# Moving small GpSimd and VectorE operations between steps of a fused SSD and gated-FFN kernel

## The chip, the cores and the metric

The kernel runs on one core of a Trainium2 chip. The metric is the device time of one execution in microseconds (us), lower is better; the time quoted is the median of several runs. A core has five engines with a queue of instructions each: TensorE (PE, matmuls; PEld is its weight load), VectorE (DVE), ScalarE (ACT), GpSimd (POOL) and SyncE (SP, which issues nearly all transfers here). Each engine works through its queue in order and waits on semaphores for the others.

## The reference

Two blocks follow each other. The first is a chunked state-space scan over `x` (4 sequences, 8 heads, 768 positions, head size 32) with decays `a` and rows `B`, `C` (state size 16):

```python
for c in range(nc):                      # chunks of 32 positions
    la = log_a[:, :, sl]
    cum = np.cumsum(la, axis=-1)
    L = np.exp(cum[:, :, :, None] - cum[:, :, None, :]) * causal
    M = np.einsum('bhin,bhjn->bhij', Cc, Bc) * L
    y_intra = np.einsum('bhij,bhjd->bhid', M, xc)
    y_inter = np.einsum('bhin,bhnd->bhid', Cc, state) * np.exp(cum)[:, :, :, None]
    y[:, :, sl] = y_intra + y_inter
    Bx = np.einsum('bhjn,bhjd->bhjnd', Bc, xc) * np.exp(cum[:, :, -1:] - cum)[:, :, :, None, None]
    state = decay_full[:, :, None, None] * state + np.sum(Bx, axis=2)
```

Its output, seen as 3072 tokens of 256 features, goes through the second block:

```python
h = x @ w_in                             # 256 -> 2048
g = h * np.cos(h)
return (g @ w_out).astype(np.float32)    # 2048 -> 256
```

All of it is in float32.

## The kernel before

The sequence of 768 positions is cut into six chunks of 128 (`NC`), each for all four sequences, so a chunk is 512 tokens. A chunk has two halves of 64 positions, called units: unit `k` is half `k % 2` of chunk `k // 2`.

**Steps.** The feed-forward block sets the beat. The loop of line 1002 has one step `n` for each block of work of the feed-forward: sixteen steps (`NF`) to a chunk, 96 in all, and two more to empty the pipeline. In step `n`, `first(n)` (line 650) multiplies activations with two blocks of 128 columns of `w_in` into a PSUM bank `hp` (two banks in turn); `wind(n)` makes, on ACT and then DVE, the argument of the cosine (`k`, `w`); `gate(n)` takes the cosine on ACT; `gated(n)` multiplies on DVE, which gives `gT` and frees the bank. Two steps later (`LAG`) `second(n - LAG)` multiplies by `w_out`. The scan block of later chunks is laid in pieces between these steps, by the table `steps` (line 916) and, for units 2 and 3, by `unit_at` (line 882).

**Seven products in place of eight.** From chunk 1 on (steps 16 and later) `second` calls `seven` (line 739), which does the 2x2 block product of `gT` with `w_out` with seven block matmuls in place of eight. It needs differences of blocks of `gT`, called `gd`, which `differ(n)` (line 707) makes on POOL at the end of `gated(n)` with three operations: L711 (256 columns), L713 and L714 (128 columns each, one after the other). It also needs four arrays of combinations of blocks of `w_out`, called `wd[0]` to `wd[3]`, made once by `differ_w(i, js)` (line 695) on POOL, operation L705; in the profile these arrays are named `words`. `js` says for which of the eight index values `j` the array is made. The order of the seven products is fixed in line 766: two of them read `gT` and `w_out` alone, the next three read `gd` from L713 and L711 and `words`; the last but one reads `gT` and `words`, and the last reads L714's result.

The dictionary `differ_at` (line 877) says in which step each `differ_w` is issued, at the step's end before `second`: the first four values of `j` (`fore`) for all four arrays in steps 14 and 15, the last four (`hind`) of arrays 0 to 3 in steps 16, 17, 18 and 19. `seven(16 + j)`, of step `18 + j`, is the first to read index `j`.

**Operations of the scan block around it.** `decays0(k, p)` (line 368) is a scan on DVE, L375, that makes the products of decays `lam` of sequence pair half `p` of unit `k`. `weigh0(k)` (line 379) makes `sc`, the rows of `B` times the decay to the unit's end, on POOL, L381; it reads `lam` of both `p`. `sums` (line 468) multiplies `sc` with `x` on TensorE, L477, to what the unit adds to the state. `reaches(c, b)` (line 567) makes `reach`, the running product of decays of sequence `b` of chunk `c`, with two short scans on DVE, L574. For chunk 1, unit 3: `turn_unit(3)` (line 434) comes in step 18, `inner(3)` (line 449, L456) at the end of step 20, followed at once by the sums of unit 4, and `finish0(3)` at the end of step 22.

**The order within a step.** The order of each engine's queue is the order in which the code issues. The work of the scan block for a step is gathered into the list `behind`. Its first entry is issued before `gated(n)`, the others after:

```python
            if not joins and behind:
                behind.pop(0)()
            if n == NF + 3:
                weigh0(4)
            gated(n)
```

`first_decays` (line 920) puts the scans of unit 4 in steps 17 and 18 and those of unit 5 in steps 19 and 20, each as the first entry. `decays2` (line 932) follows the second scan of a unit with the load of a decay row two units on (`load_arow`, which for an odd unit includes a small POOL memset) and, for units above 5, with `weigh0`. The `sc` of units 4 and 5 are issued by lines 1050 and 1055 in steps 19 and 23.

Of the kernel before, what the change touches and what calls it, by code (L numbers as in the profile page):

```python
# [25 lines left out]
def kernel(  # L26
# [18 lines left out]
    NC = S // P  # L45
    DM, DF = moe_w_in.shape
    KT = DM // P
    NF = DF // P
# [70 lines left out]
    def load_x(k, s, eng=nc.sync):  # L119
        if k not in xrs:  # L120
            t = loads.tile([P, 2, 2, H, D], FP32, tag="xr", name="xr")
            xrs.update({k // 2 * 2 + i: t[:, i] for i in range(2)})
        eng.dma_start(out=xrs[k][s * W:(s + 1) * W].rearrange("p q h d -> p (q h) d"),
                      in_=x[2 * s:2 * s + 2, :, k * W:(k + 1) * W, :]
                      .rearrange("b h i d -> i (b h) d"))

    def load(c, i):
        if c < NC:
            for s in range(2):
                (load_x if i in (1, 2) else load_b)(2 * c + i // 2, s)  # L130
# [26 lines left out]
    def load_arow(k):  # L157

        arows[k] = t = rows.tile([P, H, P], FP32, tag="arow", name="arow").rearrange(
            "p h i -> p (h i)").rearrange("p (q h i) -> p q h i", q=2, h=H)  # L160
        i = k % 2
        if i:
            G.memset(t[:, :, :, 0:1], 0.0)
        for s in range(2):
            nc.sync.dma_start(
                out=t[s * W:(s + 1) * W, :, :, i:].rearrange("p q h i -> p (q h) i"),
                in_=a_cut[2 * s:2 * s + 2, :, k * W + i:(k + 1) * W].rearrange("q h i -> (q h) i")
                .unsqueeze(0).to_broadcast([W, 2 * H, W - i]))
# [186 lines left out]
    reach, part, yT, after = {}, {}, {}, {}  # L355
# [12 lines left out]
    def decays0(k, p, i=0, n=1):  # L368

        if p == i == 0:  # L370
            lams[k] = scan.tile([P, 2, H, W], FP32, tag="lam", bufs=4, name="lam")
        flat = "p h i -> p (h i)"
        hs = slice(i * H // n, (i + 1) * H // n)
        rows_ = spread.pop((k, p, i)) if k < 2 else arows[k][:, p]
        V.tensor_tensor_scan(out=lams[k][:, p, hs].rearrange(flat), data0=rows_.rearrange(flat),  # L375
                             data1=unit0[:, hs].rearrange(flat), initial=0.0,
                             op0=ALU.mult, op1=ALU.add)

    def weigh0(k):
        scs[k] = sc = scan.tile([P, 2 * H, N], FP32, tag="sc0", bufs=3, name="sc0")  # L380
        G.tensor_tensor(out=sc, in0=bs[k].rearrange("p q (h n) -> p (q h) n", h=H),  # L381
                        in1=lams[k].rearrange("p q h i -> p (q h) i")[:, :, W - 1:W]
                        .to_broadcast([P, 2 * H, N]), op=ALU.mult)
# [183 lines left out]
    def reaches(c, b):  # L567

        s, p = divmod(b, 2)
        if p == 0:  # L570
            reach[c, s] = scan.tile([P, 2, P], FP32, tag="reach", name="reach")
        for k in range(2):
            i = slice(k * W, (k + 1) * W)
            V.tensor_tensor_scan(out=reach[c, s][:, p, i], data0=along[c][:, b, i],  # L574
                                 data1=ones[:, 0:W], initial=1.0, op0=ALU.mult, op1=ALU.mult)
# [67 lines left out]
    NJ = NF // 2  # L643
# [226 lines left out]
    def store_a(dst, src):  # L870
# [2 lines left out]


    piece = {n: ("in", (n + 3) // 2) if n % 2 else ("out", n // 2) for n in range(NF)}
    fore, hind = slice(0, NJ // 2), slice(NJ // 2, NJ)
    differ_at = {NF - 2: [(0, fore), (1, fore)], NF - 1: [(2, fore), (3, fore)],
                 **{NF + i: [(i, hind)] for i in range(4)}}

# [40 lines left out]
    def chunks_at(n, what):  # L922
        return [(c, i) for c, at in steps.items() for i, f in
                enumerate(at[what] if isinstance(at[what], tuple) else (at[what],))
                if NF * (c - 1) + f == n]
# [6 lines left out]
    def decays2(k, p):  # L932
        decays0(k, p)
        if p == 1:
            if k + 2 < 2 * NC:
                load_arow(k + 2)
            if 5 < k < 2 * NC - 1:
                weigh0(k)

    def reaches2(c, s):  # L940
        for b in (2 * s, 2 * s + 1):
            reaches(c, b)

    block_loads = {9 if c == 2 else NF * (c - 2) + 4: c for c in range(2, NC)}

# [56 lines left out]
    for n in range(AHEAD, NC * NF + LAG):  # L1002
        c, f = divmod(n, NF)
        if n < NC * NF:

            if c > 0 and f in (loads_of := (6, 7, 8, 9) if c == 1 else (0, 1, 2, 3)):
                load(c + 2, loads_of.index(f))
            if n in (NF - 4, NF - 3):
                load_arow(n - NF + 8)
            if n == NF - 2:  # L1010
                for k in (4, 5):
                    for s in range(2):
                        load_x(k, s)
            if n in (NF - 1, NF):
                load_along(2, (2 * (n == NF), 2 * (n == NF) + 1))
            for e, i in chunks_at(n, "along"):
                load_along(e + 1, (2 * i, 2 * i + 1))
            first(n)
            closing = f == NF - 1 and 1 <= c < NC - 1
            take_y = finish2(c + 1) if closing else None  # L1020
            wind(n)
            if closing:
                take_y(0)
            for e, s in chunks_at(n - 1, "turn"):
                turn2(e, s)
            for k in units_at(n, 2):
                turn_unit(k)
            if n + 1 in piece:
                rests_of.append(grade(*piece[n + 1], later=True))
            gate(n)  # L1030
            while len(rests_of) > (n == AHEAD):
                rest = rests_of.pop(0)
                if rest:
                    rest()
            joins = n in piece and piece[n] in held
            if joins:
                join(*piece[n])

            behind = [lambda at=at: decays2(*at) for at in decays_at(n)]
            behind += [lambda k=2 * c - 1 + i: add_state(k) for c, i in chunks_at(n, "state")]  # L1040
            behind += [lambda at=at: reaches2(*at) for at in chunks_at(n, "reach")]
            behind += [lambda at=at: turn_blocks(*at) for at in chunks_at(n, "turn")]
            behind += [lambda k=k, p=p: decays0(k, p) for k, at in unit_at.items()
                       for p in range(2) if at[0][p] == n]
            behind = [lambda k=2 * c + i, q=q: weights(k, q) for c, i in chunks_at(n, "weigh")
                      for q in range(2)] + behind
            behind = [lambda k=k: weights(k, 1) for k in units_at(n - 1, 3)] + behind
            if not joins and behind:
                behind.pop(0)()
            if n == NF + 3:  # L1050
                weigh0(4)
            gated(n)
            if closing:
                take_y(1)
            if n == NF + 7:
                weigh0(5)
            if add_s and (n == NF - 5 or units_at(n - 1, 4)):
                exchange = add_s()
                add_s = None
            if n == NF + 9:  # L1060
                exchange()
            for do in behind:
                do()
            if f not in ((10, 11, 12) if c == 1 else (10, 11)):
                for do in unsummed:
                    do()
                unsummed.clear()
            for k, ((_, last_), *_) in unit_at.items():
                if last_ == n:
                    weigh0(k)  # L1070
        for i, js in differ_at.get(n, ()):
            differ_w(i, js)
        if n == AHEAD + 1:
            second(AHEAD - LAG)
        if n >= LAG and n != AHEAD:
            second(n - LAG)
        for e, _ in chunks_at(n, "inner"):
            inner2(e)
        for k in units_at(n, 3):
            for t in range(2):  # L1080
                inner(k, t)
            if k == 3:
                at = [gs[k, s][:, 0, 2 * P:] for s in range(2)]
                sums(4, at, group)
                take_sums((4,), at)
            weights(k, 0)
        for k in units_at(n, 4):
            take_s, add_s = finish0(k)
            take_s()
        for k in units_at(n, 1):  # L1090
            reach_unit(k)
        if f == NF - 3 and 1 <= c < NC - 1:
            open2(c + 1)
        for at, e in block_loads.items():
            if at == n:
                loading = load_blocks(e)
            if at <= n < at + 12:
                next(loading)
# [30 lines left out]
```

## Time and profile before

| what | value |
|---|---|
| time, median of 3 runs | 369.34 us (369.16 to 369.66) |
| the profiled execution | 369.48 us |
| its span | 367.1 us |
| granted TensorE clock | 1.00 |
| data moved | 26.39 MB in 97324 packets |
| `hp` matmuls, L659 | 768, 182.7 us busy, 381 ns each |
| `seven` matmuls, L767 | 1106 in five groups |
| POOL L711, L713, L714 | 79 each: 759, 477 and 538 ns mean |
| DVE scans L375 | 20, 1489 ns mean |

The span is the time between the first and the last instruction of the profiled execution; its device time is 2.4 us longer. Each engine's busy time is the sum of its instructions; a busy TensorE isn't TensorE at its peak, since the ends of its matmuls are modelled. A mean in such a row can hide two kinds of instruction, those that ran alone and those that were held up by another engine, so single instructions are read from the timeline. The step numbers don't stand in the profile: step 16's `hp` begins at 71.82 us, step 17's at 75.28, step 18's at 78.73, step 19's at 82.45, step 20's at 86.24, step 21's at 92.59.

### The profile page before, as it was taken

To read this page: it belongs to the slowest core of one execution; us is meant where nothing else is said; L and a number is where in the kernel's file an instruction comes from. 1 tells how busy PE (TensorE), PEld (TensorE's weight loads), DVE (VectorE), ACT (ScalarE), POOL (GpSimd) and SP (SyncE) were. 2 spreads that over 40 slices of the span, in tenths; PEclk is the share of its full clock that TensorE was granted. 3 is DMA by queue.
4 is the path that set the end of the run, shared out by engine and by line. 5 is a ranking of instruction groups with operands and counts; after the bars stand their busy time and mean duration, and the time that the engine had idled before them with its cause. 6 is when DMAs were issued, how large, how long until landed. Compare 5 with 4: busy or idle time off the path is not lost.

```text
span 367.1 us, 9745 instructions
## 1 busy us (share of the span) xinstructions
PE 359.7 (98%) x3902; PEld 324.6 (88%) x3902; DVE 249.8 (68%) x420; ACT 178.0 (48%) x324; POOL 204.0 (56%) x327
## 2 busy tenths in 40 slices
PE   8999999998999999999999999999999999999995
PEld 5788888897899999999989999989999999999995
DVE  7789998588776857967735967654876463544463
ACT  4588766453354355525345444435553534444442
POOL 6567666679756553537734545744454443554451
PEclk9999999999999999999999999999999999999999
DMA  8987967682735445315125211010000010010011
GB/s 144 299 328 159 196 135 86 116 120 67 139 56 76 91 94 88 57 48 104 25 49 71 44 49 25 2 41 7 17 16 0 2 30 2 2 29 3 0 29 30
DMA packets 97324, 26.39 MB, mean 72 GB/s; under 512 B 87328, under 2 KB 93184, under 8 KB 97280
## 3 DMA queue, kind: packets, MB, share of 16 engines
q1 hardware_dynamic: 96032, 25.38, 34.3%
q8 instruction: 31, 0.51, 0.6%
q10 hardware_dynamic: 1248, 0.39, 0.5%
q14 instruction: 13, 0.11, 0.1%
HBM read 22.36 MB, written 3.34 MB: 70 GB/s over the span
## 4 chain that ended last, share of the span: by engine, by line
PE 88%; DVE 4%; POOL 4%; ACT 2%; issue 2%; POOLq 0%; ACTq 0%; DVEq 0%
PE hp L659 41%; PE o L767 33%; PE o L729 5%; PE y L629 2%; PE g L603 1%; POOL gd L711 1%; POOL words L705 1%; DVE mag L261 1%; PE y L477 1%; PE y L617 1%; DVE mag L263 1%; PE warm L84 1%; PE a_ps L364 1%; DVE w L672 1%; POOL sc L381 1%
## 5 line engine op out<-in xcount | busy, mean ns | idle before, releaser
L659 PE MATMUL hp<-yT,w_in 128*128 128x256 f32 x768 | 182.7, 381 | 0.4 <-DVE gT L686 0.4
L659 PEld LDWEIGHTS hp<-yT,w_in 128*128 128x128 f32 x768 | 139.5, 190 | 18.2 <-issue 1.0
L711 POOL TENSOR_TENSOR gd<-gT 128x256 f32<-128x256 f32 x79 | 60.0, 759 | 114.3 <-DVE gT L686 109.2
L672 DVE SCALAR_TENSOR_TENSOR w<-hp,k 128x512 f32<-128x512 f32 x96 | 66.1, 689 | 75.0 <-ACT k L666 74.9
L666 ACT ACTIVATE k<-hp 128x512 int32<-128x512 f32 x96 | 57.2, 596 | 96.4 <-PE hp L659 95.9
L681 ACT ACTIVATE w<-w,quarter 128x512 f32<-128x512 f32 x96 | 69.4, 723 | 70.2 <-DVE w L672 70.0
L686 DVE TENSOR_TENSOR gT<-hp,w 128x512 f32<-128x512 f32 x96 | 65.7, 684 | 33.2 <-ACT w L681 31.2
L767 PE MATMUL o<-words,gd 128*128 128x128 f32 x474 | 66.0, 275 | 0.6 <-POOL gd L713 0.6
L767 PEld LDWEIGHTS o<-words,gd 128*128 128x128 f32 x474 | 59.3, 192 | 1.0 <-POOL gd L713 1.0
L767 PEld LDWEIGHTS o<-w_out,gT 128*128 128x128 f32 x316 | 47.2, 191 | 4.1
L767 PE MATMUL o<-w_out,gT 128*128 128x128 f32 x316 | 48.4, 276 | 0.0
L714 POOL TENSOR_TENSOR gd<-gT,gd 128x128 f32<-128x128 f32 x79 | 42.5, 538 | 6.2
L713 POOL TENSOR_TENSOR gd<-gT,gd 128x128 f32<-128x128 f32 x79 | 37.7, 477 | 6.2
L767 PE MATMUL o<-words,gT 128*128 128x128 f32 x158 | 30.6, 275 | 0.0
L767 PE MATMUL o<-w_out,gd 128*128 128x128 f32 x158 | 30.5, 275 | 0.0
L729 PE MATMUL o<-w_out,gT 128*128 128x256 f32 x128 | 29.9, 379 | 0.0
L375 DVE TENSOR_TENSOR_SCAN lam<-arow,unit 128x512 f32<-128x512 f32 x20 | 29.8, 1489 | 0.0
L729 PEld LDWEIGHTS o<-w_out,gT 128*128 128x128 f32 x128 | 24.2, 190 | 3.3
L767 PEld LDWEIGHTS o<-w_out,gd 128*128 128x128 f32 x158 | 24.0, 192 | 0.0
L767 PEld LDWEIGHTS o<-words,gT 128*128 128x128 f32 x158 | 24.0, 192 | 0.0
L465 DVE TENSOR_TENSOR m<-g,lam 128x512 f32<-128x512 f32 x24 | 16.1, 680 | 1.5 <-ACT state L489 1.0
L784 DVE TENSOR_TENSOR sum<-ps,sum 128x256 f32<-128x256 f32 (+1 forms) x27 | 16.7, 645 | 0.6
(109 smaller groups left out, 271.4 us busy)
## 6 DMA issues: line engine op xcount, KB each, us to landing
words<-in_moe_w_in_dram SPq DMA_DIRECT2D x8, 512.0 KB
words<-in_moe_w_out_dram SPq DMA_DIRECT2D x8, 512.0 KB
xr<-in_x_dram SPq DMA_DIRECT2D x24, 128.0 KB
arow<-a_cut SPq DMA_DIRECT2D x10, 256.0 KB
arow<-a_cut SPq DMA_DIRECT2D x10, 252.0 KB
out_dram<-sum SPq DMA_DIRECT2D x18, 128.0 KB
bc<-in_B_dram SPq DMA_DIRECT2D x24, 64.0 KB
blocks<-in_B_dram SPq DMA_DIRECT2D x16, 32.0 KB
```

Source lines behind the costliest of these rows:

```text
L375: V.tensor_tensor_scan(out=lams[k][:, p, hs].rearrange(flat), data0=rows_.rearrange(flat), data1=unit0[:, hs].rearrange(flat), initial=0.0 ...
L659: PE.matmul(to_[:, e], lhsT=w_in[:, k, fs], rhs=y[:, k], start=(k == 0), stop=(k == KT - 1), skip_group_check=True)
L666: ACT.activation(k, hp[n], AF.Copy, bias=0.25, scale=INV_2PI)
L672: V.scalar_tensor_tensor(out=w, in0=hp[n], scalar=INV_2PI, in1=k, op0=ALU.mult, op1=ALU.subtract)
L681: ACT.activation(cos, cos, AF.Sin, bias=quarter, scale=TWO_PI)
L686: V.tensor_tensor(out=gT[n], in0=hp.pop(n), in1=cos, op=ALU.mult)
L711: G.tensor_tensor(out=d[:, 0:2], in0=g[:, 1:2].to_broadcast([P, 2, P]), in1=g[:, 3::-3], op=ALU.subtract)
L713: G.tensor_tensor(out=d[:, 2], in0=g[:, 0], in1=d[:, 0], op=ALU.subtract)
L714: G.tensor_tensor(out=d[:, 3], in0=g[:, 2], in1=d[:, 2], op=ALU.subtract)
L729: PE.matmul(o[c, u][:, t], lhsT=g[:, 2 * e + t], rhs=w_out[:, 2 * j + e], start=(j == e == t == 0), stop=(j == NJ - 1 and e == 1), skip_gr ...
L767: PE.matmul(at[q], lhsT=a_[q], rhs=w[q], start=(j == 0 and q in starts), stop=(j == NJ - 1), skip_group_check=True)
L784: V.tensor_tensor(out=dst, in0=a_, in1=b_.to_broadcast([P, dst.shape[1], P]), op=ALU.add)
```

## The change

There are three edits, and no operation of the computation is added or left out.

The combinations of `w_out` for the last four index values are made in two parts of two values each. The first part (`mid`, `j` 4 and 5) takes the places that `hind` had, steps 16 to 19. The second (`hind`, `j` 6 and 7) is made in steps 20, 21 and, for arrays 2 and 3, 22.

`sc` of unit 4 is issued in step 18, right after the second scan of unit 4 in `decays2`, and no longer in step 19 ahead of `gated(19)`. In step 18 `decays2` is the entry that is issued before `gated(18)`, and so `sc` stands ahead of `differ(18)` in POOL's queue.

The reach of a chunk is issued one sequence at a time. The helper `reaches2`, which did two sequences as one entry of `behind`, is gone; each sequence is now an entry of its own. Where reach is the first entry, one sequence goes before `gated(n)` and the other after it. In step 21 another entry (`weights(3, 1)`) is first, and both sequences stay after `gated`.

```diff
-    fore, hind = slice(0, NJ // 2), slice(NJ // 2, NJ)
+    fore, mid, hind = slice(0, NJ // 2), slice(NJ // 2, 3 * NJ // 4), slice(3 * NJ // 4, NJ)
     differ_at = {NF - 2: [(0, fore), (1, fore)], NF - 1: [(2, fore), (3, fore)],
-                 **{NF + i: [(i, hind)] for i in range(4)}}
+                 **{NF + i: [(i, mid)] for i in range(4)},
+                 NF + 4: [(0, hind)], NF + 5: [(1, hind)], NF + 6: [(2, hind), (3, hind)]}
...
-            if 5 < k < 2 * NC - 1:
+            if k != 5 and k < 2 * NC - 1:
                 weigh0(k)
-
-    def reaches2(c, s):
-        for b in (2 * s, 2 * s + 1):
-            reaches(c, b)
...
-            behind += [lambda at=at: reaches2(*at) for at in chunks_at(n, "reach")]
+            behind += [lambda c=c, b=2 * s + p: reaches(c, b) for c, s in chunks_at(n, "reach")
+                       for p in range(2)]
...
-            if n == NF + 3:
-                weigh0(4)
             gated(n)
```

## The prediction

> **What bounds the kernel now.** I read the page's busy shares and its chain of waits first, then TensorE's own waits before and after 93 us, then the timelines of TensorE (PE), GpSimd (POOL) and VectorE (DVE) around the stalls. The page:
>
> ```profile
> PE 359.7 (98%) x3902; PEld 324.6 (88%) x3902; DVE 249.8 (68%) x420; ACT 178.0 (48%) x324; POOL 204.0 (56%) x327
> ...
> PE 88%; DVE 4%; POOL 4%; ACT 2%; issue 2%; POOLq 0%; ACTq 0%; DVEq 0%
> ```
>
> TensorE is busy for 98% of the span, and 88% of the chain of waits is TensorE. So an edit on POOL or DVE counts only where TensorE waits for it. The waits of TensorE from 93 us to the end hold no row at all; those from 66 to 93 us (us in total, times, longest) are:
>
> ```profile
> PE g L477 <- POOL sc L381: 1.3, 1, 1.3
> PE o L767 <- POOL gd L713: 0.6, 2, 0.3
> ```
>
> Both are waits for POOL, in the steps that the change touches. TensorE's timeline there (start, length, engine, line):
>
> ```profile
> 82.45 1.89 PE L659 MATMUL hp<-yT,w_in 128*128 128x256 f32 x8
> 84.18 0.61 PE L767 MATMUL o<-w_out,gT 128*128 128x128 f32 x4
> 85.02 0.94 PE L767 MATMUL o<-words,gd 128*128 128x128 f32 x6 [0.23 <-POOL gd L713]
> ...
> 87.97 0.61 PE L767 MATMUL o<-w_out,gT 128*128 128x128 f32 x4
> 88.92 0.94 PE L767 MATMUL o<-words,gd 128*128 128x128 f32 x6 [0.35 <-POOL gd L713]
> ...
> 90.23 0.72 PE L456 MATMUL g<-cT,turned 32*64 32x128 f32 x32
> 92.20 0.46 PE L477 MATMUL g<-xr,sc 64*32 64x64 f32 x32 [1.25 <-POOL sc L381]
> ```
>
> Each `hp` group (L659) opens a step; this one is step 19, and the block L767 that follows is `seven(17)`. Undisturbed, `seven` takes 1.56 us start to start (80.89 to 82.45, 94.42 to 95.98), its `gd` matmuls coming 0.45 after its first. Here `seven(17)` runs 84.18 to 86.24, 0.50 too long, and `seven(18)` 87.97 to 90.23; before a block of small matmuls 1.66 is normal (97.71 to 99.37), so 0.60 too long. Then `inner` of unit 3 is done at about 90.88 (32 small matmuls take 0.65 start to start) and the sums of unit 4 start at 92.20, 1.32 late. Together 2.42 us: the most that can be won in this place.
>
> POOL's queue there:
>
> ```profile
> 80.46 1.03 POOL L381 TENSOR_TENSOR sc<-bc,lam 128x256 f32<-128x256 f32 x1
> 81.45 1.28 POOL L705 TENSOR_TENSOR words<-w_out 128x512 f32<-128x512 f32 x1
> 82.68 1.75 POOL L711 TENSOR_TENSOR gd<-gT 128x256 f32<-128x256 f32 x1
> 84.51 0.46 POOL L713 TENSOR_TENSOR gd<-gT,gd 128x128 f32<-128x128 f32 x1
> ...
> 85.46 1.27 POOL L705 TENSOR_TENSOR words<-w_out 128x512 f32<-128x512 f32 x1
> 86.69 1.65 POOL L711 TENSOR_TENSOR gd<-gT 128x256 f32<-128x256 f32 x1
> ...
> 89.36 1.28 POOL L705 TENSOR_TENSOR words<-w_out,words 128x512 f32<-128x512 f32 x1
> 90.59 1.56 POOL L381 TENSOR_TENSOR sc<-bc,lam 128x256 f32<-128x256 f32 x1
> ```
>
> and the scans on DVE:
>
> ```profile
> 82.69 1.21 DVE L375 TENSOR_TENSOR_SCAN lam<-arow,unit 128x512 f32<-128x512 f32 x1
> ...
> 85.68 2.13 DVE L375 TENSOR_TENSOR_SCAN lam<-arow,unit 128x512 f32<-128x512 f32 x1
> ...
> 89.46 2.25 DVE L375 TENSOR_TENSOR_SCAN lam<-arow,unit 128x512 f32<-128x512 f32 x1
> ```
>
> POOL has no gap from 80.46 to 97 us: it is the bound of this stretch. `gT(17)` was ready at 80.30 (DVE L686, 79.63 for 0.67), but its `differ` starts at 82.68, behind `sc` and a combination of `w_out` (L705).
>
> **What the Trainium skill says.** "SBUF — State Buffer", section "Who interferes with whom": a DVE instruction with two SBUF inputs contends with a GpSimd instruction that reads SBUF; the section "SBUF: two separate sides" adds that the first to start keeps the shared ports for its whole instruction and the other blocks. The trace agrees. The scan at 85.68 waits for L705's end at 86.73 and ends at 87.81, 1.08 after; the one at 89.46 ends 1.07 after L705. In turn L711 of 82.68 and 86.69 end 0.53 after the scans, and the last `sc` 0.44 after. Free of this, a scan takes 1.21, L711 0.73 (92.11) and `sc` 0.64 (120.36).
> "GPSIMD Engine Reference", section "3.1 Elementwise": a two-input operation costs about 2.6 cycles an element at 1.2 GHz, 2.2 ns. The trace: 512 columns in 1.27, 256 in 0.73, so 2.1 ns a column and 0.19 fixed. "Perfetto Trace Analysis", section "GPSIMD Engine Instruction", advises start-to-start spacing rather than spans; L705 then costs 1.24.
>
> **The change part by part.** The order of instructions of both programs shows no difference on TensorE, ACT or SP: no transfer is moved. On POOL four L705 of 512 columns become eight of 256, and `sc` of unit 4 moves from ahead of `differ(19)` to ahead of `differ(18)`. On DVE only the reach scans move.
>
> A 256-column L705 isn't in the trace; `sc` (same columns) bounds it below with 0.64, L711 above with 0.73. I take 0.70 between starts. Walking POOL's queue:
>
> Step 17. The first part runs 81.45 to 82.15, so L711 of `differ(17)` starts at 82.15 and ends at 82.88, where before it met the scan of 82.69. That scan now waits for L711, 82.88 + 1.08 = 83.96 (0.06 later than before). L713 waits for it and ends 0.26 after, at 84.22 (0.26 as in 78.70, where it ended at 79.97 behind a scan that ended at 79.71). TensorE wants `gd` at 84.18 + 0.45 = 84.63: no stall, 0.50 won. `seven(17)` ends at 85.74, `hp(20)` at 85.74 + 1.73 = 87.47.
>
> Step 18. L714 ends about 84.75, the second part runs 84.71 to 85.40, `sc` of unit 4 85.40 to 86.04 (its scan ended at 83.96). The scan of 85.68 waits for it: 86.04 + 1.08 = 87.12 instead of 87.81. L711 of `differ(18)` ends at 87.12 + 0.53 = 87.65, L713 at 88.18 (0.07 between them), TensorE goes on 0.05 later, 88.23. It wanted 87.47 + 0.45 = 87.92. From the late `gd` to the next block the trace has 1.31 (88.92 to 90.23), so `inner` of unit 3 starts at 89.54, 0.69 before the old 90.23.
>
> Step 20. `sc` has been there since 86.04, so the sums of unit 4 follow at 89.54 + 0.65 = 90.19 instead of 92.20. Won in all: 2.0 us of the 2.42; a part of the stall at `seven(18)` stays. I take 1.95, as 0.05 is the grain of these sums.
>
> What is late next? Part three runs 88.67 to 89.37, the scan of unit 5 after it to 90.45, L711 of `differ(19)` to 90.98, L713 to 91.51; `seven(19)` wants it at 92.48 + 0.45 = 92.93. In hand 1.4. Part four of the first halves ends near 92.8; `seven(20)`, the first to read it, comes at 97.71 - 1.95 = 95.8. The second halves end in step 22: its `differ` follows `gT(22)`, 100.92 - 1.95 - 0.5 = 98.5, is done near 100.2, and two L705 end it at 101.7; `seven(22)` reads them at 106.38 - 1.95 = 104.4. The four more instructions cost 8 x 0.70 - 4 x 1.24 = 0.64 of POOL; they fall where POOL waits 0.76 (before 97.70) and 1.49 (before 101.06) today. Without that cover, each would delay a `gd` by up to 0.70, still less than its slack.
>
> The reach scans: in step 22 and once or twice in each later chunk `gT` comes two scans earlier (2 x 0.26 = 0.5), the second sequence one `gT` (0.66) later. TensorE has no wait row there, so neither is worth anything; the reach is read in the next step, over 2 us on. Zero.
>
> Later steps are a shift: after 93 us TensorE waits for nobody, so 1.95 won at 92 us lasts if no transfer is late. The profiled execution took 369.48 around a span of 367.1, 0.14 above the median 369.34; less 1.95 it is 367.5, and the median 367.4.
>
> **The rivals.** B, only a part arrives. `sc` ahead of `differ(18)` sits in a tight place: the second part of L705 ends 0.28 before the scan of 85.68 arrives. If POOL is that much later the scan goes first, to 86.8, `sc` ends at 87.2, L713 at 88.5, and 1.7 is won. With L705 and `sc` also costing more, or `seven(17)` still stalling for its 0.5, it is 1.1: 368.2.
> C, it is given back by 108 us. SP issues without pause from 67 to 99 us, so the last load of `blocks` for chunk 2 (issued 97.55 to 99.10) doesn't come earlier with TensorE. Its transposes ran at 104.75 without waiting and would now be due at 102.8. If the load lands only at 104.7, then `gT`, `w` and `rT` behind it put `inner2` at 107.4 instead of 107.94, and 0.5 is left: 368.9. Against it: the DMA share falls to 0.07 from 102 to 104 us, so it had landed.
> D, slower. `sc` of unit 4 now stands ahead of `differ(18)`, and also waits for its B rows. Before, the first proof that they had arrived is 90.59. If they come late, POOL and all behind it stop in step 18. `sc`, L711 and L713 take 0.64 + 0.73 + 0.07 + 0.46 = 1.9 and the sums follow 2.0 after L713, so from a start at 88.3 on it loses; at 90 us it costs 1.7: 371.0. Against it: they were issued at 60.14 to 63.53, and the decay rows issued behind them on SP at 67.53 fed a scan at 78.50 that didn't wait.
>
> **How the numbers follow.** A 0.70, 367.4 (own range 366.9 to 367.8: with no stall left at `seven(18)` 2.42 is won, with the scan first 1.7). B 0.16, 368.2. C 0.08, 368.9. D 0.06, 371.0. A change of 0.2%, 0.74 us, is about what a measurement of this kernel can tell from none. So faster 0.86, same 0.08, slower 0.06. The range holds A and most of B: 366.8 to 368.3.
>
> **What would show it.** Right: no POOL wait at `seven(17)`; one of about 0.3 at `seven(18)`; no wait of the L477 matmuls for `sc`; these at 90.2 and the next `hp` at 90.6; the scan of step 19 ending near 87.1; after 93 us no TensorE wait. Wrong: `sc` waiting for a transfer, L713 of `differ(18)` ending after 88.6, or a new TensorE wait between 93 and 110 us.

## The result, and the profile after

The changed kernel took 367.85 us (median of 20 runs, 367.37 to 369.42) and the kernel before, run beside it, 369.41 us (20 runs). The ratio is 0.9958 with a 95% interval of 0.9950 to 0.9967: 1.56 us less, by the interval 1.2 to 1.85. The profiled execution took 367.37 us with a span of 365.2; it is the fastest of the twenty, whose spans have a median of 365.65.

The page of the changed kernel, busy shares and chain of waits by engine:

```profile
PE 359.7 (98%) x3902; PEld 324.8 (89%) x3902; DVE 249.6 (68%) x420; ACT 177.8 (49%) x324; POOL 204.5 (56%) x331
...
PE 89%; DVE 4%; POOL 3%; ACT 2%; issue 2%; ACTq 0%; POOLq 0%; DVEq 0%
```

TensorE's work is the same, 359.7 us; the span is shorter by waiting alone, and of the chain one hundredth has gone from POOL to TensorE. TensorE has no wait row left after 66 us. Its timeline in steps 19 and 20 (start, length):

```profile
84.13 0.61 PE L767 MATMUL o<-w_out,gT 128*128 128x128 f32 x4
84.58 0.83 PE L767 MATMUL o<-words,gd 128*128 128x128 f32 x6
...
87.42 0.61 PE L767 MATMUL o<-w_out,gT 128*128 128x128 f32 x4
88.11 0.94 PE L767 MATMUL o<-words,gd 128*128 128x128 f32 x6
...
89.42 0.72 PE L456 MATMUL g<-cT,turned 32*64 32x128 f32 x32
90.07 0.49 PE L477 MATMUL g<-xr,sc 64*32 64x64 f32 x32
90.49 1.99 PE L659 MATMUL hp<-yT,w_in 128*128 128x256 f32 x8
```

`gd` follows 0.45 after the start of `seven(17)`, the undisturbed distance; at `seven(18)` it is 0.69, so a stall stays there, too short to be given a wait row. The sums of unit 4 follow `inner` after 0.65 with no wait. POOL, and the scans on DVE, in the same stretch:

```profile
80.76 1.12 POOL L705 TENSOR_TENSOR words<-w_out 128x256 f32<-128x256 f32 x1
81.84 0.73 POOL L711 TENSOR_TENSOR gd<-gT 128x256 f32<-128x256 f32 x1
82.64 1.46 POOL L713 TENSOR_TENSOR gd<-gT,gd 128x128 f32<-128x128 f32 x1
...
84.59 0.73 POOL L705 TENSOR_TENSOR words<-w_out 128x256 f32<-128x256 f32 x1
85.28 0.65 POOL L381 TENSOR_TENSOR sc<-bc,lam 128x256 f32<-128x256 f32 x1
85.87 1.65 POOL L711 TENSOR_TENSOR gd<-gT 128x256 f32<-128x256 f32 x1
87.60 0.45 POOL L713 TENSOR_TENSOR gd<-gT,gd 128x128 f32<-128x128 f32 x1
```

```profile
82.64 1.21 DVE L375 TENSOR_TENSOR_SCAN lam<-arow,unit 128x512 f32<-128x512 f32 x1
...
85.63 1.37 DVE L375 TENSOR_TENSOR_SCAN lam<-arow,unit 128x512 f32<-128x512 f32 x1
...
88.92 1.44 DVE L375 TENSOR_TENSOR_SCAN lam<-arow,unit 128x512 f32<-128x512 f32 x1
```

L711 of `differ(17)` ends at 82.57, before the scan of 82.64 asks for the SBUF port that POOL and DVE share; only the short L713 has to wait for that scan. In step 18 `sc` holds the port to 85.93, the scan of 85.63 gets it then and ends at 87.00, and L711 ends at 87.52, 0.52 after. That is the chain `sc`, scan, L711, L713 behind the stall that stays.

### The profile page after: what moved, and what is told of

It reads as the page before. It is cut to its first block, busy times and chain, and to the rows that moved or that the text cites. A ratio compares the mean times of both kernels' runs of the same rounds, so it can differ in the third digit from the quotient of the medians.

```text
span 365.2 us, 9749 instructions
## 1 busy us (share of the span) xinstructions
PE 359.7 (98%) x3902; PEld 324.8 (89%) x3902; DVE 249.6 (68%) x420; ACT 177.8 (49%) x324; POOL 204.5 (56%) x331
## 4 chain that ended last, share of the span: by engine, by line
PE 89%; DVE 4%; POOL 3%; ACT 2%; issue 2%; ACTq 0%; POOLq 0%; DVEq 0%
PE hp L659 42%; PE o L767 33%; PE o L729 5%; PE y L629 2%; PE g L603 1%; PE y L477 1%; DVE mag L261 1%; PE y L617 1%; DVE mag L263 1%; POOL gd L711 1%; PE g L456 1%; PE a_ps L364 1%; PE warm L84 1%; DVE w L672 1%; POOL gd L713 1%
## 5 line engine op out<-in xcount | busy, mean ns | idle before, releaser
L711 POOL TENSOR_TENSOR gd<-gT 128x256 f32<-128x256 f32 x79 | 59.8, 757 | 111.9 <-DVE gT L686 102.5
L767 PE MATMUL o<-words,gd 128*128 128x128 f32 x474 | 65.9, 275 | 0.1
L767 PEld LDWEIGHTS o<-words,gd 128*128 128x128 f32 x474 | 59.3, 192 | 0.3 <-POOL gd L713 0.3
L767 PEld LDWEIGHTS o<-w_out,gT 128*128 128x128 f32 x316 | 47.2, 191 | 4.1
L767 PE MATMUL o<-w_out,gT 128*128 128x128 f32 x316 | 48.4, 276 | 0.0
L714 POOL TENSOR_TENSOR gd<-gT,gd 128x128 f32<-128x128 f32 x79 | 44.0, 557 | 6.2
L713 POOL TENSOR_TENSOR gd<-gT,gd 128x128 f32<-128x128 f32 x79 | 38.1, 483 | 6.2
L767 PE MATMUL o<-words,gT 128*128 128x128 f32 x158 | 30.6, 275 | 0.0
L767 PE MATMUL o<-w_out,gd 128*128 128x128 f32 x158 | 30.6, 275 | 0.0
L375 DVE TENSOR_TENSOR_SCAN lam<-arow,unit 128x512 f32<-128x512 f32 x20 | 28.0, 1400 | 0.0
L767 PEld LDWEIGHTS o<-words,gT 128*128 128x128 f32 x158 | 24.0, 192 | 0.0
L767 PEld LDWEIGHTS o<-w_out,gd 128*128 128x128 f32 x158 | 24.0, 192 | 0.0
L784 DVE TENSOR_TENSOR sum<-ps,sum 128x256 f32<-128x256 f32 (+1 forms) x27 | 15.1, 586 | 0.6
```

The source lines that it names most:

```text
L711: G.tensor_tensor(out=d[:, 0:2], in0=g[:, 1:2].to_broadcast([P, 2, P]), in1=g[:, 3::-3], op=ALU.subtract)
L713: G.tensor_tensor(out=d[:, 2], in0=g[:, 0], in1=d[:, 0], op=ALU.subtract)
L714: G.tensor_tensor(out=d[:, 3], in0=g[:, 2], in1=d[:, 2], op=ALU.subtract)
L767: PE.matmul(at[q], lhsT=a_[q], rhs=w[q], start=(j == 0 and q in starts), stop=(j == NJ - 1), skip_group_check=True)
```

## The experiments

The starts of the profiles differ by up to 1.0 us at step 18 (78.43 to 79.42), so a single span says less than a distance within it. I use the distance from the start of `hp(18)` to the sums of unit 4 (L477), which holds all three stalls: 13.47 us in the kernel before, 11.39 after. Times are medians, each beside runs of the kernel before on the same chip (369.24 to 369.45 us). The ratio is not that of the two medians: like a ratio of means it moves with every run, and a few long ones raise it. The medians of e1_halves alone would give 0.9953, but four of its 22 runs lie above 369 us.

| kernel | `hp(18)` to sums | us | ratio to before, 95% interval |
|---|---|---|---|
| e1_halves | 11.05 | 367.51 | 0.9964, 0.9949 to 0.9979 |
| e2_sc | 13.32 | 369.48 | 1.0006, 0.9997 to 1.0016 |
| e3_reach | 13.25 | 369.33 | 1.0003, 0.9994 to 1.0012 |
| e5_halves_sc | 11.44 | 367.89 | 0.9980, 0.9956 to 1.0004 |
| e9_after (the change once more) | 11.43 | 367.90 | 0.9962, 0.9949 to 0.9975 |
| e7_sc_after | 11.05 | 367.73 | 0.9965, 0.9951 to 0.9980 |
| e6_whole_late | 11.05 | 370.84 | 1.0040, 1.0025 to 1.0055 |
| e8_sc_twice | 12.04 | 368.74 | 0.9983, 0.9976 to 0.9991 |
| e10_after_sp | 11.44 | 368.15 | 0.9970, 0.9953 to 0.9986 |
| e11_sc_after_sp | 11.05 | 367.61 | 0.9945, 0.9933 to 0.9958 |
| e12_before_sp | 13.01 | 369.73 | 1.0014, 0.9998 to 1.0031 |

### One part of the change alone

**e1_halves**, the first edit alone:

```diff
-    fore, hind = slice(0, NJ // 2), slice(NJ // 2, NJ)
+    fore, mid, hind = slice(0, NJ // 2), slice(NJ // 2, 3 * NJ // 4), slice(3 * NJ // 4, NJ)
...
-                 **{NF + i: [(i, hind)] for i in range(4)}}
+                 **{NF + i: [(i, mid)] for i in range(4)},
+                 NF + 4: [(0, hind)], NF + 5: [(1, hind)], NF + 6: [(2, hind), (3, hind)]}
```

> Only the combinations of w_out in two parts; sc of unit 4 stays in step 19, reach two sequences at a time. Theory Q (POOL's backlog in steps 17 and 18, with the port shared with DVE deciding the order): walking POOL's queue, differ(17) and differ(18) are both in time, sc of unit 4 is done at 89.3 us where TensorE wants it at 89.7, so all three stalls go: 2.4 us won in the span, about 0.35 more than with the whole change. Rival S (the place of sc carries the gain, as the longest wait row names it): sc stays behind, so its wait of 1.3 us stays and at most 1.1 us are won.

Measured: 11.05 us to the sums, 2.42 less than before, no stall in any of the three places. POOL in steps 18 and 19 of this kernel:

```profile
84.90 0.73 POOL L705 TENSOR_TENSOR words<-w_out 128x256 f32<-128x256 f32 x1
85.58 0.73 POOL L711 TENSOR_TENSOR gd<-gT 128x256 f32<-128x256 f32 x1
86.39 1.25 POOL L713 TENSOR_TENSOR gd<-gT,gd 128x128 f32<-128x128 f32 x1
...
88.82 0.64 POOL L381 TENSOR_TENSOR sc<-bc,lam 128x256 f32<-128x256 f32 x1
```

L711 runs at once, at 85.58, ahead of the scan of step 19 (85.89 here), and `sc`, in its old place, is done at 89.46, 0.53 before the sums start at 89.99. The longest wait row of the kernel before named `sc`, but `sc` was only where the backlog showed. Theory Q stands, rival S falls. The time fell by 1.73 us in the medians (1.35 in e5 below, on the same chip); by the ratios, whose intervals overlap, this kernel and the whole change can't be told apart.

**e2_sc**, the second edit alone:

```diff
-            if 5 < k < 2 * NC - 1:
+            if k != 5 and k < 2 * NC - 1:
...
-            if n == NF + 3:
-                weigh0(4)
```

> Only sc of unit 4 moved from step 19 to step 18; combinations whole. Theory Q: seven(17) stalls as before (0.5); sc ends at 88.25 us behind the scan of step 19, L713 of differ(18) at 89.5, so seven(18) stalls longer than before by 0.6 and the sums of unit 4 start at 91.5 instead of 92.2: 0.7 us won. Rival S: the wait of 1.3 us goes, 1.3 to 2 us won.

Measured: no gain in the time, 0.15 us in the distance. Its TensorE and POOL in step 20:

```profile
89.63 0.94 PE L767 MATMUL o<-words,gd 128*128 128x128 f32 x6 [0.94 <-POOL gd L713]
```

```profile
86.80 1.56 POOL L381 TENSOR_TENSOR sc<-bc,lam 128x256 f32<-128x256 f32 x1
88.32 0.72 POOL L711 TENSOR_TENSOR gd<-gT 128x256 f32<-128x256 f32 x1
89.12 0.45 POOL L713 TENSOR_TENSOR gd<-gT,gd 128x128 f32<-128x128 f32 x1
89.65 1.39 POOL L714 TENSOR_TENSOR gd<-gT,gd 128x128 f32<-128x128 f32 x1
```

The wait for `sc` goes and the wait for `gd` takes its place, as Q said (L713 at 89.57, expected 89.5). What Q left out is L714: it meets the next scan (DVE, 89.58) and ends at 91.04, and the last of the seven products waits 0.3 for it. From the late `gd` to the next block TensorE takes 1.88 (89.63 to 91.51) where 1.31 is the rule, and that 0.57 is most of the 0.66 by which the sums come later than expected (92.16, not 91.5). So the move of `sc` is worth nothing by itself.

**e3_reach**, the third edit alone:

```diff
-            behind += [lambda at=at: reaches2(*at) for at in chunks_at(n, "reach")]
+            behind += [lambda c=c, b=2 * s + p: reaches(c, b) for c, s in chunks_at(n, "reach")
+                       for p in range(2)]
```

> Only reach one sequence at a time. Theories Q and S: TensorE waits for nothing after 93 us, so no change: within 0.2 us of before, gT of step 22 earlier by about 0.5 us in the trace. Rival R (reach in front of gT costs time in each chunk): up to 4 times 0.5 us won.

Measured: a ratio of 1.0003 (0.9994 to 1.0012), so at most about 0.2 us is won where rival R had up to 2. The expected earlier `gT` did not come: in step 22 it starts at 100.20, in the kernel before at 100.23. With two scans fewer ahead of it, it waits 0.33 for the cosine from ACT:

```profile
100.20 0.69 DVE L686 TENSOR_TENSOR gT<-hp,w 128x512 f32<-128x512 f32 x1 [0.33 <-ACT w L681]
```

**e5_halves_sc** is the other side, the two diffs of e1 and e2 together and no reach edit.

> The whole change without the reach edit. Theories Q and S: as the whole change, 1.6 to 2.1 us won, a wait of about 0.25 us at seven(18). Rival R: less than the whole change by what reach brings.

Measured: 11.44 us to the sums, as with the reach edit (11.39 and 11.43). Its few runs leave a wide interval, so the time alone doesn't decide; with e3 beside it rival R has nothing to stand on.

### The place of sc, and its price

**e7_sc_after** puts `sc` of unit 4 behind `differ(18)`:

```diff
-            if k != 5 and k < 2 * NC - 1:
+            if 5 < k < 2 * NC - 1:
...
             gated(n)
+            if n == NF + 2:
+                weigh0(4)
```

> The whole change, but sc of unit 4 behind differ(18) in step 18 instead of ahead of it. Theory Q: the last stall at seven(18) goes as well, since L711 of differ(18) then runs before the scan of step 19 asks for the port; sc is done near 88.4 us, 1.3 before the sums need it. From hp(18) to the sums 11.05 us as in the halves-only kernel, where the whole change has 11.39: some 0.35 us less than the whole change. Rival V (the difference of 0.35 between those two profiles is scatter of a single execution): 11.4 as in the whole change.

and **e9_after**, the changed kernel once more, with no edit:

> The changed kernel once more, beside the variants on the same chip. Theory Q: 11.4 us from hp(18) to the sums, a stall of about 0.35 at seven(18), 1.6 to 2 us less than before. Rival V: 11.0 to 11.7 by chance.

Measured: 11.05 in e7, the stall at `seven(18)` is gone; 11.43 in e9. `seven(18)` on TensorE and L711 of `differ(18)` on POOL, in e7:

```profile
87.24 0.61 PE L767 MATMUL o<-w_out,gT 128*128 128x128 f32 x4
87.69 0.83 PE L767 MATMUL o<-words,gd 128*128 128x128 f32 x6
```

```profile
85.15 0.73 POOL L711 TENSOR_TENSOR gd<-gT 128x256 f32<-128x256 f32 x1
```

L711 starts 0.30 before the scan of step 19 (DVE, 85.45). The 0.34 to 0.39 between the kernels is the place of `sc` and no scatter: the four profiles with `sc` ahead of `differ(18)` once and the smaller parts (after, e5, e9, e10) have 11.39 to 11.44, the three with the smaller parts and `sc` behind it (e1, e7, e11) 11.05 each. The times are less clear. The medians of e7 and e9, 367.73 and 367.90, are too close to tell apart with five runs of e9. The medians of the spans are lower with `sc` behind in each pair on one chip: e1 365.2 and e5 365.5, e7 365.4 and e9 365.6, e11 365.0 and e10 365.55, with 5 to 22 runs each. The traced execution of e7 had a new stall later, which the last group deals with.

**e8_sc_twice** makes `sc` of unit 4 twice, ahead of `differ(18)`:

```diff
         scs[k] = sc = scan.tile([P, 2 * H, N], FP32, tag="sc0", bufs=3, name="sc0")
-        G.tensor_tensor(out=sc, in0=bs[k].rearrange("p q (h n) -> p (q h) n", h=H),
+        for _ in range(2 if k == 4 else 1):
+            G.tensor_tensor(out=sc, in0=bs[k].rearrange("p q (h n) -> p (q h) n", h=H),
```

> The whole change with sc of unit 4 made twice, one after the other, in its place ahead of differ(18); the second writes the same values. Theory Q: the scan of step 19 takes the port between the two, L713 of differ(18) is 0.6 us later and the stall at seven(18) grows by as much: 12.0 us from hp(18) to the sums, 0.6 more than the whole change in all. Rival W (POOL has room there and the stall is set by the scan alone): no change from the whole change.

Measured: 12.04, 0.61 to 0.65 more than the whole change, as Q expected; the medians of the two sets beside each other differ by 0.84 us in the time and 0.6 in the span. POOL, the scan and TensorE (the edit adds a line to the kernel, so L382, L714 and L768 are the L381, L713 and L767 of the others):

```profile
85.89 2.16 POOL L382 TENSOR_TENSOR sc<-bc,lam 128x256 f32<-128x256 f32 x2
```

```profile
86.20 1.42 DVE L375 TENSOR_TENSOR_SCAN lam<-arow,unit 128x512 f32<-128x512 f32 x1
```

```profile
89.32 0.94 PE L768 MATMUL o<-words,gd 128*128 128x128 f32 x6 [0.73 <-POOL gd L714]
```

The scan of 86.20 ends at 87.62, between the two. The second `sc`, 0.64 where it runs alone, is paid for by TensorE at its full length.

### Size of the pieces, or room in the queue

**e6_whole_late** leaves the pieces whole and issues them two steps later:

```diff
-                 **{NF + i: [(i, hind)] for i in range(4)}}
+                 **{NF + 2 + i: [(i, hind)] for i in range(4)}}
```

> Before, but the four whole combinations of the last four index values in steps 18 to 21 instead of 16 to 19; sc and reach as before. Theory Q: room in POOL's queue in steps 16 to 18 is what counts, not the size of the pieces: the three stalls up to the sums go (11.0 to 11.1 us from hp(18) to the sums), but the last array is ready only near 98.9 us, some 2.4 after seven(20) asks for its index 4, so a new stall of 2 to 2.5 us stands at seven(20) in step 22 and the whole is within 0.5 us of before. Rival P (the smaller pieces themselves free the port sooner): the old stalls at seven(17) and seven(18) stay or move by the same size, 12.5 us or more to the sums.

Measured: 11.05 to the sums, so room in the queue is enough and the size of the pieces isn't needed for it. The new stall is where it was expected. TensorE, in step 22:

```profile
96.13 0.94 PE L767 MATMUL o<-words,gd 128*128 128x128 f32 x6
99.15 0.49 PE L767 MATMUL o<-words,gT 128*128 128x128 f32 x2 [2.08 <-POOL words L705]
```

The two halves of the first edit thus do two things: fewer columns early make room, and the early half is there when index 4 and 5 are due. The time was worse than expected, by 1.57 us over before instead of within 0.5. In the traced execution step 22 took 8.06 us instead of 5.11 and step 23 4.33 instead of 3.39, which takes back the 2.42 won and 1.47 more; a part of this is a fall of the clock, told in the last section. The clock isn't all of it: the five executions that kept the full clock lay 0.5 to 1.4 us above the median of before as well, and why is open.

### What the sooner TensorE runs into

In the profile of the changed kernel DVE waits for a transfer that it did not wait for before; the other profile of the same kernel, e9, has no such wait. Its transposes of the second half of chunk 2 (L582):

```profile
102.69 0.64 DVE L582 STREAM_TRANSPOSE turned<-blocks 128x256 f32<-128x256 f32 x1
104.12 0.67 DVE L582 STREAM_TRANSPOSE turned<-blocks 128x256 f32<-128x256 f32 x1 [0.79 <-DMA blocks<-in_C_dram]
```

In e7_sc_after the same wait was 1.84 us and reached TensorE. Its DVE and TensorE:

```profile
104.61 0.65 DVE L582 STREAM_TRANSPOSE turned<-blocks 128x256 f32<-128x256 f32 x1 [1.84 <-DMA blocks<-in_C_dram]
```

```profile
105.24 0.45 PE L603 MATMUL g<-cT,turned 32*64 32x128 f32 x8
106.25 1.14 PE L603 MATMUL g<-cT,turned 32*64 32x128 f32 x56 [0.56 <-ACT cT L591]
```

From one `hp` to the next that step took 5.46 us where 4.52 is normal, 0.94 lost. When SP issues the last piece of this load scatters: at 97.55 us in the kernel before, 98.37 in e9, 98.54 in the changed kernel, 100.48 in e7. The test issues it sooner:

```diff
-    block_loads = {9 if c == 2 else NF * (c - 2) + 4: c for c in range(2, NC)}
+    block_loads = {8 if c == 2 else NF * (c - 2) + 4: c for c in range(2, NC)}
...
-            if n == NF - 2:
-                for k in (4, 5):
-                    for s in range(2):
-                        load_x(k, s)
+            if n in (NF - 2, NF + 5):
+                for s in range(2):
+                    load_x(4 if n == NF - 2 else 5, s)
```

**e10_after_sp**, this edit on the changed kernel:

> The whole change, with the last load of blocks for chunk 2 issued earlier: its pieces start one step earlier and the load of x of unit 5 goes from step 14 to step 21, behind them. Theory B2 (the transposes of the blocks of chunk 2 wait for their load now that TensorE comes 2 us sooner, which takes part of the gain in some executions): the wait of VectorE for the load, 0.79 us in the profile of the changed kernel, is gone, and the median falls by 0.2 to 0.5 us. Rival N (VectorE's wait has cover in every execution, and the smaller gain in the median than in the profile is scatter elsewhere): the wait goes, the median stays within 0.15 us of the changed kernel.

**e11_sc_after_sp**, on e7:

> As the kernel with sc behind differ(18), with the same earlier load of blocks. Theory B2: the stall of 0.56 us at the g matmuls of chunk 2 goes, no TensorE wait is left from 66 us on, and it is the fastest: 2.3 to 2.5 us less than before, 366.8 to 367.0. Rival N: 367.4 to 367.7, as the kernels without a stall at seven(18) had.

**e12_before_sp**, on the kernel before:

> Before, with the earlier load of blocks alone. Both theories: in the kernel before, the transposes of the second half of chunk 2 come at 104.75 us and wait for nothing, so no change, within 0.2 us.

Measured: e12 is the same as before (1.0014, with 1 in its interval; 0.28 us more in the medians, where at most 0.2 was expected). DVE's wait is gone in e10 and e11, and so is TensorE's in e11. But e10's median did not fall (368.15 in 6 runs, against 367.90 in 5 runs for the change in e9; the spans have 365.55 and 365.6), so B2 missed and rival N holds for the changed kernel: the load was late there, and TensorE had cover. The 0.25 by which e10 is higher is more than N allowed, but the intervals of the two ratios overlap widely. e11 is the kernel with the lowest ratio, 0.9945; its median of 367.61, of 5 runs, is where rival N had it (367.4 to 367.7), not where B2 had it (366.8 to 367.0). Its interval overlaps that of the change (0.9933 to 0.9958 against 0.9950 to 0.9967). Its trace has no TensorE wait after 66 us and 11.05 to the sums. That it beats the change is shown for that distance, not for the time.

## Why the prediction was right, point by point

**The bound.** Right. All that was won lies in the three stalls of steps 19 and 20: 13.47 less 11.39 is 2.08 us. Behind them 0.2 was lost again: from the sums to TensorE's last group of matmuls it is 269.39 us (90.07 to 359.46) instead of 269.19 (92.20 to 361.39).

**Step 17.** Right: L711 before the scan, no stall. The whole stretch ran about 0.3 sooner than in the walk, since `sc` of unit 3 met no scan this time (0.64 long instead of 1.03; the part of L705 behind it met one, 1.12 instead of 0.73).

**Step 18.** Right in mechanism and size: `sc`, then the scan, then L711 at scan end plus 0.53 (measured 0.52), L713 late. The remaining delay of `gd` was put at 88.23 - 87.92 = 0.31 and measured as 0.24. What I did not draw from this walk is that the second edit costs 0.35 us of TensorE once the first is made; e1, e7 and e11 show it in the distance. So the first edit carries the gain, and no run shows a gain from the other two.

**Step 20.** Right: `sc` no longer ends anything, and what was put at 2.0 in all was 2.08 in the profile.

**Four more POOL instructions, reach, later slack.** Right, all three at zero: the later halves lie at 94.39, 97.43 and 100.82 us with no TensorE wait, and e3 measures reach as nothing. The price was right, but the reason given with it, that `gT` of step 22 comes 0.5 sooner, was not: e3 has it where it was.

**The size.** 1.95 was predicted, 1.56 measured (1.2 to 1.85), so the predicted gain is outside the interval. The time of 367.85 us is in the stated range, but just above A's own (366.9 to 367.8) and nearer to B's 368.2 than to A's 367.4, though the trace shows the mechanism of A. That the range took in most of B helped.

One term that was mis-sized is the first, "0.50 won" at `seven(17)`. It was read from one execution, and some executions with the same order in these steps lose less there. In e12_before_sp TensorE runs

```profile
84.21 0.61 PE L767 MATMUL o<-w_out,gT 128*128 128x128 f32 x4
84.66 0.86 PE L767 MATMUL o<-words,gd 128*128 128x128 f32 x6
```

with no stall: L711 of `differ(17)` starts at 82.46, ahead of the scan of 82.72, where in the profile of before it came at 82.68 beside a scan of 82.69 and lost. In e3_reach the two are just as close and L711 wins:

```profile
82.88 0.73 POOL L711 TENSOR_TENSOR gd<-gT 128x256 f32<-128x256 f32 x1
```

```profile
82.89 1.80 DVE L375 TENSOR_TENSOR_SCAN lam<-arow,unit 128x512 f32<-128x512 f32 x1
```

In e2_sc, whose order is the same up to here, both come at 82.81 and it loses. So `seven(17)` lost 0.50, 0.49, 0.27 and 0.02 in the four profiles (before, e2, e3, e12), 0.32 in the mean: a race, in which recorded starts 0.01 apart do not tell who wins. With the smaller part L711 was 0.5 to 0.8 ahead of that scan in every profile, and the race is over. Over the three profiles that keep `sc` in step 19 (before, e3, e12) the distance is 13.47, 13.25 and 13.01, mean 13.24; the four with the step-18 place of `sc` (after, e5, e9, e10) have 11.39 to 11.44, mean 11.42. That is 1.82 to win.

The spans on record agree with it: their medians are 365.6 in e9, 365.5 in e5 and 365.55 in e10, beside 367.4, 367.3 and 367.3 for before, so 1.75 to 1.8 less. The medians of the times in the same sets fell by 1.30 to 1.37. So some 0.4 of the gain in the span is not seen in the time: the time outside the span was longer with these kernels, and why is open. The prediction took the time to fall with the span. For the 20 runs of before beside the result no spans are on record, so for 1.56 itself this is likely and not shown.

**The rivals.** B's mechanism, the scan ahead of `sc` in step 18, is in none of the four profiles of that order. Its walk has a slip: a scan of 1.21 from 85.68 ends at 86.89, not 86.8. C's first half came true: the load of `blocks` was late, by 0.79 us for DVE. My argument against it, that the DMA share had fallen to 0.07 by 102 us, was worth little: that is a figure of one execution of the kernel before. In the changed kernel SP issued the last piece at 98.54 to 100.07, 1 us later than there, and DVE waited for it until 104.12. C's second half, that it takes the gain back, did not come true here; in one execution of e7 0.94 was taken back. D did not come: `sc` waited for no transfer.

## What to carry to other kernels

The longest wait can name where a backlog shows and not what made it: walk the queue of the engine that is waited for, instruction by instruction, and ask which of them could come later. An instruction moved ahead of another on a full queue is paid for by what stands behind it, so a move that is needed with one order may cost with another. When a stall ends by a race of a few tenths, read more than one execution before its length goes into a sum, and when the bound engine comes sooner, look at the transfers that don't.

## What the hardware showed unexpectedly

Not expected was what a pause of TensorE cost in e6_whole_late. Its windows after the stall of 2.08 us (after the six busy times: granted clock, DMA share, GB/s):

```profile
100.00:102.00 2.00, 2.00 (x129) 1.76 (x121) 1.40 (x3) 0.17 (x1) 1.33 (x3) 0.62 0.49 60
102.00:104.00 2.00, 2.00 (x6) 1.64 (x6) 0.00 (x0) 1.01 (x4) 0.31 (x1) 0.53 0.13 29
```

The granted clock fell to 0.62 and 0.53 for some 4 us, and the next step took 4.33 us instead of 3.39. Of the 11 runs six had a mean clock of 0.995, as this one, and took 370.84 to 371.91 us; five had 1.000 and took 369.78 to 370.67. By the mean clock the fall comes in about half of the executions, and the means of the two groups are 1.0 us apart; only this execution is traced. Single runs of other kernels have such a clock too (0.994 with 371.34 us in e1, 0.995 with 371.97 in e5 and 371.42 in e7), and what made it fall there is not known. The Trainium skill, "TensorE: Matmul & The Clock Gate", Part 1, puts the return to half clock after an idle window of about 3.4 us. The trace differs from it: a wait of 2.08 was enough in this execution, where the product that waited came 2.35 after it was due. In the kernel before, the wait of 1.25 left the clock at 1.00:

```profile
90.00:92.00 2.00, 0.95 (x35) 0.59 (x33) 2.00 (x2) 0.30 (x1) 2.00 (x2) 1.00 0.51 120
92.00:94.00 2.00, 1.79 (x39) 1.55 (x40) 0.99 (x2) 0.93 (x4) 1.84 (x5) 1.00 0.24 53
```
